# Decay attention and two gated layers: the attention's result in 32-column parts of the array, scores and state update in one burst, and a re-ordered plan

## The chip, the cores and the metric

The kernel runs on one core of one Trainium2 chip. A core has a matmul engine (TensorE, in the profile PE, its weight loads PEld), VectorE (DVE), ScalarE (ACT), GpSimd (POOL) and SyncE (SP), which issues the DMA transfers. The metric is the device time of one execution in microseconds; lower is better. Before the change the median of three runs is 1067.16 us (1066.91 to 1067.5).

## What is computed

Three stages follow each other, all in float32. The attention keeps a 48x48 state for each of 4 batches and 8 heads over 768 time steps:

```python
for t in range(S):
    kt, vt, rt = (k[:, :, t], v[:, :, t], r[:, :, t])
    cur = np.einsum('bhd,bhe->bhde', u[None] * kt, vt)
    y[:, :, t] = np.einsum('bhd,bhde->bhe', rt, state + cur)
    state = w[None, :, :, None] * state + np.einsum('bhd,bhe->bhde', kt, vt)
```

Its output, 3072 tokens of 384 numbers, goes through two gated layers with 1536 hidden columns:

```python
xn = x / rms * rms_g
x = silu(xn @ w_gate) * (xn @ w_val) @ w_out           # first layer
x = sigmoid(x @ w_gate2) * (x @ w_val2) @ w_out2       # second layer
```

The weights arrive as float64; the kernel turns them into pairs of float32 numbers itself.

## The kernel before, in words

**Attention.** The 768 steps of each batch are cut into 6 chunks of 128; a chunk of one batch is a tile, 24 tiles in all, taken chunk by chunk over the batches (tiles 0 to 3 are the first chunks, 20 to 23 the last). In a tile, keys and queries are scaled by powers of the decay (`kq`, `rq`, with `wk` and `wr`) and turned (`kT`, `rT`: in tiles 1 to 7 by TensorE, from tile 8 on by VectorE transposes and DMA). TensorE then runs four bursts, each with its own place in the order:
- `scores` (L498): 8 matmuls, for 4 pairs of heads, the two heads of a pair in the upper and lower 64 rows of the array. VectorE masks the two banks into `aa` (L502).
- `from_state` (L511), not in the first chunk: 4 matmuls of a head pair's `rT` with `zb`, a copy of the state `z` in which the two heads of a pair stand on a block diagonal (zeros elsewhere). ScalarE makes this copy in two pieces per tile (L539).
- `from_tile` (L518): 8 matmuls of `aa` with `vn`, into the same bank; VectorE adds `vc` and writes `x` (L521).
- `update` (L528), not in the last chunk: 8 matmuls of `kq` with `vn`, 48 columns of the array each, even heads in the left and odd heads in the right half. VectorE adds the product to `z` (L535) and multiplies it by `wc`.

Every float32 matmul of these leaves two records in the trace. `x` is then normalised, turned and split into a high and a low part, `xh` and `xl`.

**Gated layers.** A block is 512 tokens, six blocks per layer; a step is one block with 128 of the 1536 hidden columns, so 12 steps to a block and 144 in all. A step of the first layer has 9 + 9 matmuls of 512 columns for gate and value (L668 to L670) and 9 for the output (L695), 27 in all. ScalarE makes the gate (L675), VectorE the product (L677), ScalarE and VectorE split it into `hh` and `hl` (L679, L680). Step 11 is the last of block 0. Block 0 needs attention tiles 0 to 3, block 1 tiles 4 to 7, and so on. During block 0 the weights of each step are converted too (ScalarE L63, L68, L630; VectorE L77, L78, L633; GpSimd L84).

**What sets the order.** Nothing is scheduled on the chip. Class `Plan` places every task with an estimated duration, a due time, the data it reads and writes, and its PSUM banks, and writes each engine's instructions in the order that this gives. `DUE` sets when a tile of block 0, 1 and later blocks falls due (offset before its block, distance between tiles; a step is 3 units), `LEAD` how early the parts of a weight conversion are due, `STEP` how early a step's vector work is due. Tokens such as `("v", n)` name what tasks wait for. A task's token `("v", n)` stands for step n's value bank, and attention also names its ring of three value tiles `("v", 0)` to `("v", 2)`.

Of the kernel before, what the change touches and what calls it, by code (L numbers as in the profile page):

```python
# [11 lines left out]
AF = mybir.ActivationFunctionType  # L12
ALU = mybir.AluOpType
AX = mybir.AxisListType

P = 128
HS = 112
NPAIR = 4
# [6 lines left out]
DUE = (-59, 4), (-47, 4), (-42, 8)  # L25


LEAD = 15, 10, 7, 7, 8, 9
STEP = 4
# [69 lines left out]
class Plan:  # L99
# [46 lines left out]
    def run(self, start, fly):  # L146
# [18 lines left out]
        for _ in self.tasks:  # L165
            best = None
            for e, waiting in engines.items():

                first, could = None, []
                for n in waiting:  # L170
                    us, _, _, _, psum, dma = self.tasks[n]
# [3 lines left out]
                    at = at[e]  # L175
# [17 lines left out]
            at, n, e = best  # L193
# [33 lines left out]
def blocked(  # L227
# [31 lines left out]
    def ring(name, n, shape, dtype=F32):  # L259
        return [work.tile(shape, dtype, name=f"{name}{i}") for i in range(n)]  # L260
# [25 lines left out]

    zb = ring("zb", B, [HS, NPAIR, 2 * D])
# [38 lines left out]
    def setup():  # L326


        for t in zb:
            nc.gpsimd.memset(t, 0.0)  # L330
# [126 lines left out]
    def attention(i):  # L457
# [37 lines left out]
        def scores(*sp):  # L495
# [3 lines left out]
        add("T", 1.1, d + 3, scores, [(t, i2, n) for t in ("kT", "rT") for n in range(2)],  # L499
            [name("sp")], psum=[name(("sp", n)) for n in range(2)], gate=[("aa", n) for n in range(2)])  # L500
# [11 lines left out]
        if not first:  # L512
            add("T", 0.7, d + 5, from_state, [("rT", i2, n) for n in range(2)] + [("zb", b, 0), ("zb", b, 1)], [name("yp")],
                psum=[name("yp")], gate=[("x", i2)])
# [5 lines left out]
        add("T", 0.9, d + 6, from_tile, [("aa", 0), ("aa", 1), ("v", i3)], [name("yp")], psum=[name("yp")], gate=[("x", i2)])  # L520
        add("V", 0.47, d + 7, lambda yp: nc.vector.tensor_tensor(  # L521
            out=x[i2], in0=yp[:, :DM], in1=flat(vc[i2]), op=ALU.add), [name("yp"), ("vc", i2)], [("x", i2)], psum=[name("yp")])


        if not last:
            def update(up):
                for h in range(H):
                    nc.tensor.matmul(up[rows(h % 2), h // 2 * D:(h // 2 + 1) * D], kq_[:, h, :], vn[i3][:, h, :], start=True, stop=True)  # L528
            u3 = lambda up: up[:HS, :NPAIR * D].rearrange("p (q e) -> p q e", q=NPAIR)
            add("T", 0.55, d + 8, update, [("kq", i2), ("v", i3)], [name("up")], psum=[name("up")], gate=[("z", b)])  # L530
# [3 lines left out]
            else:  # L534
                add("V", 0.27, d + 9, lambda up: nc.vector.tensor_tensor(out=z[b], in0=u3(up), in1=z[b], op=ALU.add),  # L535
                    [name("up")], [("z", b)], psum=[name("up")])
                add("VG", (0.27, 0.55), d + 9, either(z[b], z[b], wc, ALU.mult), ["wc"], [("z", b)])
# [121 lines left out]
    def step(n, bi, f):  # L659
# [4 lines left out]
        def hidden(kind):  # L664
# [11 lines left out]
        add("T", 2.1, d + 1, hidden(1), xs + [("w", f, 1), ("g", n)], [("v", n)], psum=[("v", n)])  # L676
        add("V", 0.69, d + 1 - STEP, lambda ps: nc.vector.tensor_tensor(out=sg[n2], in0=ps, in1=sg[n2], op=ALU.mult),  # L677
            [("v", n)], [("sg", n2)], psum=[("v", n)])
# [268 lines left out]
```

## Time and profile before

| what | value |
|---|---|
| median of three runs | 1067.16 us |
| the profiled execution's own time | 1057.77 us |
| its span | 1056.0 us |
| mean granted TensorE clock | 0.992 |
| VectorE busy | 497.1 us |
| ScalarE busy | 357.9 us |
| GpSimd busy | 130.4 us |

The span runs from the first to the last instruction in the trace; 1.8 us of the execution lie around it. The share of busy time is a mean over three stages with different limits: the start until block 0 is done, the rest of the first layer with the other attention tiles between its steps, and the second layer, in which there is no attention. So each stage is read by itself below.

### The profile page before, as it was taken

The numbers are of one execution on the slowest core, as the hardware profiler recorded it, in microseconds if no ns is written. First come the engines' busy times: TensorE is split into PE (matmuls) and PEld (weight loads), VectorE is DVE, ScalarE is ACT, GpSimd is POOL, SyncE is SP. The second block draws the span as 40 slices with busy tenths as digits, with TensorE's granted clock in tenths as the row PEclk, the third lists the DMA queues.
The fourth block names the chain that finished last, engine by engine and source line by source line (L and its number), as shares of the span: only waits on it lengthen the run. The fifth ranks groups of instructions, "written<-read, shape, count | busy, mean of one in ns | idle before, by whom it ended". The sixth has DMA issues, their size and how long they took to land.

```text
span 1056.0 us, 14430 instructions
## 1 busy us (share of the span) xinstructions
PE 1034.9 (98%) x5474; PEld 870.4 (82%) x5474; DVE 497.1 (47%) x957; ACT 357.9 (34%) x750; POOL 130.4 (12%) x157
## 2 busy tenths in 40 slices
PE   7989999999999999999999999999999999999997
PEld 6867787888888888888888888888888888888886
DVE  8999984445664665554456422322322322222221
ACT  5566652223333333333455412221212212212121
POOL 4534430000121221011001000000000000000000
PEclk9989999999999999999999999999999999999998
DMA  9944755345565777543465300100100100000000
GB/s 199 254 95 131 135 121 108 60 77 136 123 153 124 158 156 163 133 126 96 145 192 165 120 1 1 60 1 1 61 1 1 60 1 1 30 1 5 27 1 34
DMA packets 213743, 91.10 MB, mean 86 GB/s; under 512 B 156576, under 2 KB 205984, under 8 KB 213664
## 3 DMA queue, kind: packets, MB, share of 16 engines
q1 hardware_dynamic: 213664, 90.08, 35.2%
q8 instruction: 45, 0.74, 0.3%
q14 instruction: 34, 0.28, 0.1%
HBM read 64.10 MB, written 25.95 MB: 85 GB/s over the span
## 4 chain that ended last, share of the span: by engine, by line
PE 89%; DVE 8%; issue 1%; ACT 1%; DMA 1%; SPq 0%; DVEq 0%; ACTq 0%
PE bank L695 27%; PE bank L668 19%; PE bank L669 18%; PE bank L670 18%; PE bank L518 3%; PE bank L498 2%; PE bank L511 1%; DVE wraw L78 1%; DVE w L633 1%; DVE wt L77 1%; DVE vc L466 1%; DVE aa L502 1%; DVE sg L314 1%; PE bank L528 1%; DVE hl L680 0%
## 5 line engine op out<-in xcount | busy, mean ns | idle before, releaser
L668 PE MATMUL bank<-xh,w 128*128 128x512 f32 x864 | 345.7, 400 | 0.6 <-ACT w L630 0.6
L669 PE MATMUL bank<-xl,w 128*128 128x512 f32 x864 | 342.1, 396 | 0.0
L670 PE MATMUL bank<-xh,w 128*128 128x512 f32 x864 | 341.9, 396 | 0.0
L677 DVE TENSOR_TENSOR sg<-bank,sg 128x512 f32<-128x512 f32 x144 | 99.4, 691 | 386.4 <-PE bank L670 386.1
L670 PEld LDWEIGHTS bank<-xh,w 128*128 128x128 f32 x864 | 162.5, 188 | 39.0 <-DVE w L633 0.5
L668 PEld LDWEIGHTS bank<-xh,w 128*128 128x128 f32 x864 | 162.7, 188 | 37.2 <-ACT w L630 1.0
L669 PEld LDWEIGHTS bank<-xl,w 128*128 128x128 f32 x864 | 162.7, 188 | 34.2
L675 ACT ACTIVATE sg<-bank 128x512 f32<-128x512 f32 x144 | 86.0, 598 | 303.5 <-PE bank L670 303.0
L679 ACT ACTIVATE hh<-sg 128x512 fp32r<-128x512 f32 x144 | 90.8, 631 | 228.8 <-DVE sg L677 228.7
L695 PE MATMUL bank<-w,hh 128*128 128x384 f32 x576 | 158.7, 337 | 0.0
L695 PE MATMUL bank<-hh,w 128*128 128x512 f32 x432 | 149.4, 399 | 0.8 <-ACT hh L679 0.8
L680 DVE TENSOR_TENSOR hl<-sg,hh 128x512 fp32r<-128x512 f32 x144 | 100.8, 700 | 62.6 <-ACT hh L679 62.5
L695 PEld LDWEIGHTS bank<-w,hh 128*128 128x128 f32 x576 | 105.1, 188 | 3.4
L695 PEld LDWEIGHTS bank<-hh,w 128*128 128x128 f32 x432 | 81.1, 188 | 20.5 <-ACT hh L679 1.2
L695 PE MATMUL bank<-w,hl 128*128 128x384 f32 x288 | 96.7, 336 | 0.0
L695 PE MATMUL bank<-hl,w 128*128 128x512 f32 x216 | 85.6, 396 | 1.9 <-DVE hl L680 1.9
L695 PEld LDWEIGHTS bank<-w,hl 128*128 128x128 f32 x288 | 54.1, 188 | 3.3 <-DVE hl L680 0.3
L84 POOL TENSOR_TENSOR wt<-wraw 128x384 int32<-128x384 int32 x36 | 32.5, 903 | 187.0 <-DVE wraw L78 110.2
L518 PEld LDWEIGHTS bank<-vn,aa 128*128 128x128 f32 x384 | 47.9, 198 | 5.9 <-DVE aa L502 3.9
L518 PE MATMUL bank<-vn,aa 128*128 128x48 f32 x384 | 48.3, 279 | 3.7 <-DVE aa L502 3.4
L63 ACT ACTIVATE wt<-wraw 128x384 f32<-128x384 f32 x72 | 39.7, 552 | 35.4 <-DMA wraw<-in_moe_w_gate_dram 11.3
L695 PEld LDWEIGHTS bank<-hl,w 128*128 128x128 f32 x216 | 40.6, 188 | 11.6 <-DVE hl L680 2.5
(121 smaller groups left out, 761.3 us busy)
## 6 DMA issues: line engine op xcount, KB each, us to landing
wraw<-in_moe_w_gate_dram SPq DMA_DIRECT2D x24, 384.0 KB, 4.0
wraw<-in_moe_w_val_dram SPq DMA_DIRECT2D x24, 384.0 KB, 4.3
wraw<-in_moe_w_out_dram SPq DMA_DIRECT2D x24, 384.0 KB, 4.5
parked<-wt SPq DMA_DIRECT2D x36, 192.0 KB, 2.7
wt<-parked SPq DMA_DIRECT2D x36, 192.0 KB, 2.4
kn<-in_k_dram SPq DMA_DIRECT2D x24, 192.0 KB, 4.4
rn<-in_r_dram SPq DMA_DIRECT2D x24, 192.0 KB, 4.5
vn<-in_v_dram SPq DMA_DIRECT2D x24, 192.0 KB, 3.4
```

Source lines behind the costliest of these rows:

```text
L63: nc.scalar.activation(t.bitcast(F32), raw[:, :, 1].bitcast(F32), AF.Abs, scale=2.0 ** -112, accum_out=total)
L84: nc.gpsimd.tensor_tensor(out=out, in0=raw[:, :, 1], in1=raw[:, :, 0], op=ALU.add)
L498: nc.tensor.matmul(sp[n][:, p * P:(p + 1) * P], kT[i2][rows(n), p, :], rT[i2][rows(n), p, :], start=True, stop=True)
L518: nc.tensor.matmul(yp[:, h * D:(h + 1) * D], aa[0][:, h % 2, h // 2, :], vn[i3][:, h, :], start=(first and h == 0), stop=True, skip_group_ ...
L668: nc.tensor.matmul(ps, whi[f][:, kind, ws], xh[b2][:, c, :], start=(c == 0), stop=False)
L669: nc.tensor.matmul(ps, whi[f][:, kind, ws], xl[b2][:, c, :], start=False, stop=False)
L670: nc.tensor.matmul(ps, wlo[f][:, kind, ws], xh[b2][:, c, :], start=False, stop=(c == KC - 1))
L675: add("A", 0.6, d - STEP, lambda g: nc.scalar.activation(sg[n2], g, gate), [("g", n)], [("sg", n2)], psum=[("g", n)])
L677: add("V", 0.69, d + 1 - STEP, lambda ps: nc.vector.tensor_tensor(out=sg[n2], in0=ps, in1=sg[n2], op=ALU.mult), [("v", n)], [("sg", n2)], ...
L679: add("A", 0.63, d + 1 - STEP, lambda: nc.scalar.activation(hh[n2], sg[n2], AF.Copy), [("sg", n2)], [("hh", n2)])
L680: add("VG", (0.69, 1.5), d + 1 - STEP, lambda e: by[e].tensor_tensor(out=hl[n2], in0=sg[n2], in1=hh[n2].bitcast(F32), op=ALU.subtract), [( ...
L695: nc.tensor.matmul(a[:, :rhs.shape[-1]], lhsT, rhs, start=(f == 0 and i == 0), stop=(f == NF - 1 and i == 2))
```

## The change

`from_state` and `from_tile` become one task, `result` (L525 and L530). Each of their matmuls is cut into four, one for each quarter of the tile's 128 steps, so that each takes 32 columns of the array. The state's share no longer uses a block diagonal: each head is a matmul with 48 rows from `z` itself, even heads in the upper and odd heads in the lower 64 rows. That makes 32 + 32 matmuls in place of 4 + 8, into two banks in place of one (even heads, odd heads); VectorE adds `vc` in two halves (L536). The copy `zb`, its zeroing on GpSimd and its ScalarE copies go. `scores` and `update` become one task, which takes three banks at once. The step's value token is renamed `("value", n)`, so it is no longer the same name as attention's value tiles. When two engines could start a task at the same moment, the plan now takes the one with the earlier due time first. `DUE`, `LEAD` and `STEP` have other numbers, and the plan's estimates for the new bursts are 1.4, 0.95, 1.6 and 1.1 us.

```diff
-DUE = (-59, 4), (-47, 4), (-42, 8)
-LEAD = 15, 10, 7, 7, 8, 9
-STEP = 4
+DUE = (-75, 4), (-36, 5), (-41, 6)
+LEAD = 17, 20, 18, 15, 14, 18
+STEP = 12
+Y_US, S_US = (1.4, 0.95), (1.6, 1.1)
...
-                _, n = min((self.tasks[n][1], n) for at, n in could if at <= first + 1e-9)
-                if best is None or first < best[0]:
-                    best = (first, n, e)
+                due, n = min((self.tasks[n][1], n) for at, n in could if at <= first + 1e-9)
+                if best is None or (first, due) < best[:2]:
+                    best = (first, due, n, e)
...
+        def both(*ps):
+            scores(*ps[:2])
+            if not last:
+                update(ps[2])
...
-        def from_state(yp):
-            y3 = yp[:, :DM].rearrange("p (q e) -> p q e", q=NPAIR)
-            for p in range(NPAIR):
-                nc.tensor.matmul(y3[:, p, :], rT[i2][:HS, p, :], zb[b][:, p, :], start=(p == 0), stop=False, skip_group_check=True)
-        def from_tile(yp):
-            for h in range(H):
-                nc.tensor.matmul(yp[:, h * D:(h + 1) * D], aa[0][:, h % 2, h // 2, :], vn[i3][:, h, :],
-                                 start=(first and h == 0), stop=True, skip_group_check=True)
+        quarters = [slice(t, t + P // 4) for t in range(0, P, P // 4)]
+        def result(*yp):
+            for p in range(NPAIR if not first else 0):
+                for ts in quarters:
+                    for n in range(2):
+                        nc.tensor.matmul(yp[n][ts, p * D:(p + 1) * D], rT[i2][rows(n), p, ts], z[b][rows(n), p, :],
+                                         start=(p == 0), stop=False, skip_group_check=True)
+            for n in range(2):
+                for p in range(NPAIR):
+                    for ts in quarters:
+                        nc.tensor.matmul(yp[n][ts, p * D:(p + 1) * D], aa[0][:, n, p, ts], vn[i3][:, 2 * p + n, :],
+                                         start=(first and p == 0), stop=True, skip_group_check=True)
...
-            for n in range(2):
-                add("A", 0.25, d + 10, lambda n=n: nc.scalar.activation(
-                    zb[b][rows(n), :, n * D:(n + 1) * D], z[b][rows(n)], AF.Copy), [("z", b)], [("zb", b, n)])
...
-        add("T", 2.1, d + 1, hidden(1), xs + [("w", f, 1), ("g", n)], [("v", n)], psum=[("v", n)])
+        add("T", 2.1, d + 1, hidden(1), xs + [("w", f, 1), ("g", n)], [("value", n)], psum=[("v", n)])
```

How the order moves is shown at three places. The first is TensorE ahead of the first gated step. Before, tile 4's result (L511, L518) is followed by tile 5's scores (L498), and the first step (L668) starts behind them; its two halves then have tile 5's and 6's attention between them:

```order
L511 MATMUL bank_77<-zb_125,rT_116 128x96 x4
L518 MATMUL bank_78<-vn_100,aa_117 128x48 x8
L498 MATMUL bank_80<-rT_116,kT_114 128x128
...
L668 MATMUL bank_79<-xh_128,w_446 128x512
...
L324 MATMUL bank_74<-ident,kq_102 112x128 x4
L324 MATMUL bank_75<-ident,rq_104 112x128 x4
L528 MATMUL bank_76<-vn_99,kq_102 48x48 x8
L518 MATMUL bank_77<-vn_101,aa_117 128x48 x8
L498 MATMUL bank_78<-rT_115,kT_113 128x128
```

After the change, tile 4's scores, update (L502) and result (L525, L530) are the last attention ahead of the first step (L678), and five more steps follow it with no attention between them:

```order
L502 MATMUL bank_73<-vn_100,kq_102 48x48 x8
L525 MATMUL bank_77<-z_120,rT_115 32x48
...
L530 MATMUL bank_77<-vn_100,aa_117 32x48 x16
L530 MATMUL bank_74<-vn_100,aa_117 32x48 x16
L574 MATMUL bank_75<-ident,x_119 128x128 x3
L678 MATMUL bank_79<-xh_124,w_435 128x512
```

Tiles 5, 6 and 7 moved from the start of block 0 into its steps 6 to 11, and tiles 8 and 9, which stood in steps 6 to 10, moved behind step 11's output.

The second place is TensorE around tile 14, deep in the first layer. Before, its scores, its two result bursts (both into bank_80) and its update stand apart, with matmuls of the gated layers (left out) between them:

```order
L498 MATMUL bank_79<-rT_115,kT_113 128x128
L498 MATMUL bank_78<-rT_115,kT_113 128x128
...
L511 MATMUL bank_80<-zb_126,rT_115 128x96 x4
...
L518 MATMUL bank_80<-vn_101,aa_117 128x48 x8
...
L528 MATMUL bank_78<-vn_101,kq_102 48x48 x8
```

After, such a tile has two places, one with scores and update, one with the result in two banks (tile 12's, then tile 13's):

```order
L525 MATMUL bank_79<-z_120,rT_115 32x48
L525 MATMUL bank_78<-z_120,rT_115 32x48
...
L530 MATMUL bank_79<-vn_99,aa_117 32x48 x16
L530 MATMUL bank_78<-vn_99,aa_117 32x48 x16
...
L498 MATMUL bank_79<-rT_116,kT_114 128x128
L498 MATMUL bank_80<-rT_116,kT_114 128x128
...
L502 MATMUL bank_78<-vn_100,kq_103 48x48 x8
```

Four entries into the row of gated matmuls became two for each tile.

The third place is VectorE up to the product of step 11 (L677, after L687). Before, 316 rows stand ahead of it, and just ahead are a state update, a conversion and a transpose for tile 9:

```order
L475 TENSOR_REDUCE cf_107<-vc_105 128x8
L466 TENSOR_TENSOR z_122<-z_122,wc 112x192
L553 SCALAR_TENSOR_TENSOR x_119<-x_119,rms_112,g_bc 128x384
L77 TENSOR_SCALAR wt_147<-wt_147 128x384
L446 STREAM_TRANSPOSE vc_106<-x_119 128x384
L78 SCALAR_TENSOR_TENSOR wraw_143<-wraw_143,wt_147 128x384
L677 TENSOR_TENSOR sg_133<-bank_76,sg_133 128x512
```

After, 284 rows stand ahead of the same product, and what is just ahead belongs to tile 7's split and tile 8's first transposes:

```order
L580 TENSOR_TENSOR xl_127<-bank_80,xh_125 128x3x128
L446 STREAM_TRANSPOSE kn_97<-kq_102 128x384
L446 STREAM_TRANSPOSE rn_95<-rq_104 128x384
L80 TENSOR_SCALAR wt_143<-wt_143 128x384
L475 TENSOR_REDUCE cf_107<-vc_105 128x8
L81 SCALAR_TENSOR_TENSOR wraw_139<-wraw_139,wt_143 128x384
L687 TENSOR_TENSOR sg_129<-bank_76,sg_129 128x512
```

Most of tiles 8 and 9 moved behind the product, and some multiplications moved to GpSimd.

## Rows read from the trace of the kernel before

**Rows 1.** The page: busy time of each engine, share of the span, instructions.

```profile
PE 1034.9 (98%) x5474; PEld 870.4 (82%) x5474; DVE 497.1 (47%) x957; ACT 357.9 (34%) x750; POOL 130.4 (12%) x157
```

**Rows 2.** By stretch: length, busy PE, PEld, DVE, ACT, POOL; clock, DMA share, GB/s.

```profile
25.00:50.00 25.00, 24.08 (x261) 20.95 (x260) 24.69 (x58) 15.01 (x40) 12.99 (x15) 1.00 1.15 248
50.00:75.00 25.00, 20.11 (x135) 17.09 (x134) 22.14 (x46) 14.85 (x39) 7.20 (x8) 0.86 0.56 140
...
11.00:163.00 152.00, 141.66 (x995) 117.34 (x995) 142.52 (x297) 94.90 (x238) 65.38 (x62) 0.97 0.71 158
163.00:599.00 436.00, 436.00 (x2297) 354.88 (x2296) 235.12 (x449) 159.41 (x340) 59.28 (x69) 1.00 0.54 132
```

**Rows 3.** TensorE's waits: who waited for whom, us in total, times, longest.

```profile
PE bank L518 <- DVE aa L502: 3.4, 4, 2.2
```

**Rows 4.** TensorE's timeline at the start: start, us, engine, line, operation, count [idle before].

```profile
29.57 1.76 PE L518 MATMUL bank<-vn,aa 128*128 128x48 f32 x14 [0.24 <-DVE aa L502]
...
60.33 3.13 PE L518 MATMUL bank<-vn,aa 128*128 128x48 f32 x14 [2.18 <-DVE aa L502]
```

**Rows 5.** Timeline of VectorE and TensorE at the end of step 11.

```profile
155.68 0.69 DVE L677 TENSOR_TENSOR sg<-bank,sg 128x512 f32<-128x512 f32 x1 [0.84 <-PE bank L670]
...
162.24 0.39 PE L695 MATMUL bank<-hh,w 128*128 128x512 f32 x1
```

**Rows 6.** TensorE's timeline: each burst with a gated matmul ahead and the second behind.

```profile
279.46 0.39 PE L695 MATMUL bank<-hh,w 128*128 128x512 f32 x1
279.69 1.03 PE L511 MATMUL bank<-zb,rT 112*128 112x96 f32 x8
...
280.81 0.39 PE L669 MATMUL bank<-xl,w 128*128 128x512 f32 x1
...
282.44 0.40 PE L670 MATMUL bank<-xh,w 128*128 128x512 f32 x1
282.68 1.88 PE L518 MATMUL bank<-vn,aa 128*128 128x48 f32 x16
...
284.69 0.39 PE L669 MATMUL bank<-xl,w 128*128 128x512 f32 x1
...
288.42 0.40 PE L695 MATMUL bank<-hh,w 128*128 128x512 f32 x1
288.75 0.56 PE L528 MATMUL bank<-vn,kq 128*48 128x48 f32 x16
...
289.58 0.39 PE L669 MATMUL bank<-xl,w 128*128 128x512 f32 x1
...
295.41 0.40 PE L695 MATMUL bank<-hh,w 128*128 128x512 f32 x1
295.74 1.16 PE L498 MATMUL bank<-rT,kT 48*128 48x128 f32 x16
...
297.17 0.40 PE L669 MATMUL bank<-xl,w 128*128 128x512 f32 x1
```

**Rows 7.** By line and shape: busy us, mean ns of one, idle before.

```profile
L518 PE MATMUL bank<-vn,aa 128*128 128x48 f32 x384 | 48.3, 279 | 3.7 <-DVE aa L502 3.4 <-DVE rms L549 0.2
...
L528 PE MATMUL bank<-vn,kq 128*48 128x48 f32 x320 | 11.4, 216 | 0.0
...
L502 DVE TENSOR_TENSOR aa<-bank,mask 128x512 f32<-128x512 f32 x48 | 31.5, 682 | 12.6 <-PE bank L498 12.6
...
L553 DVE SCALAR_TENSOR_TENSOR x<-x,rms,g_bc 128x384 f32<-128x384 f32 x24 | 16.7, 695 | 5.6 <-POOL rms L465 5.6
...
L521 DVE TENSOR_TENSOR x<-bank,vc 128x384 f32<-128x384 f32 x24 | 13.3, 553 | 37.3 <-PE bank L518 37.3
...
L475 DVE TENSOR_REDUCE cf<-vc 128x8 f32<-128x384 f32 x24 | 12.9, 538 | 0.0
...
L535 DVE TENSOR_TENSOR z<-bank,z 112x192 f32<-112x192 f32 x16 | 5.5, 350 | 1.9 <-PE bank L528 1.9
...
L549 DVE TENSOR_SCALAR rms<-ss 128x1 f32<-128x1 f32 x24 | 3.6, 148 | 7.6 <-ACT vc L544 7.3
...
L539 ACT ACTIVATE zb<-z 48x192 f32<-48x192 f32 x40 | 14.4, 360 | 14.8 <-DVE z L466 8.9 <-PE bank L511 5.6
```

More of the change, by code (lines that the diff above doesn't have):

```diff
@@ L285, in blocked @@
     x, z = ring("x", 2, [P, DM]), ring("z", B, [HS, NPAIR, D])
-    zb = ring("zb", B, [HS, NPAIR, 2 * D])
     xh, xl = ring("xh", 2, [P, KC, N], F32R), ring("xl", 2, [P, KC, N], F32R)
@@ L326, in setup @@
     def setup():
-        for t in zb:
-            nc.gpsimd.memset(t, 0.0)
         nc.vector.memset(o[0], 0.0)
@@ L498, in scores, with update @@
                     nc.tensor.matmul(sp[n][:, p * P:(p + 1) * P], kT[i2][rows(n), p, :], rT[i2][rows(n), p, :], start=True, stop=True)
-        add("T", 1.1, d + 3, scores, [(t, i2, n) for t in ("kT", "rT") for n in range(2)],
-            [name("sp")], psum=[name(("sp", n)) for n in range(2)], gate=[("aa", n) for n in range(2)])
+        def update(up):
+            for h in range(H):
+                nc.tensor.matmul(up[rows(h % 2), h // 2 * D:(h // 2 + 1) * D], kq_[:, h, :], vn[i3][:, h, :], start=True, stop=True)
+        def both(*ps):
+            scores(*ps[:2])
+            if not last:
+                update(ps[2])
+        more = [] if last else [name("up")]
+        add("T", S_US[last], d + 3, both, [(t, i2, n) for t in ("kT", "rT") for n in range(2)] + ([] if last else [("kq", i2), ("v", i3)]),
+            [name("sp")] + more, psum=[name(("sp", n)) for n in range(2)] + more, gate=[("aa", n) for n in range(2)])
         for n in range(2):
@@ L505, in attention @@
                 [name("sp")], [("aa", n)], psum=[name(("sp", n))])
-        def from_state(yp):
-            y3 = yp[:, :DM].rearrange("p (q e) -> p q e", q=NPAIR)
-            for p in range(NPAIR):
-                nc.tensor.matmul(y3[:, p, :], rT[i2][:HS, p, :], zb[b][:, p, :], start=(p == 0), stop=False, skip_group_check=True)
-        if not first:
-            add("T", 0.7, d + 5, from_state, [("rT", i2, n) for n in range(2)] + [("zb", b, 0), ("zb", b, 1)], [name("yp")],
-                psum=[name("yp")], gate=[("x", i2)])
@@ new lines, in attention @@
+        banks = [name(("yp", n)) for n in range(2)]
+        add("T", Y_US[first], d + 6, result, [("aa", 0), ("aa", 1), ("v", i3)] + ([] if first else [("rT", i2, 0), ("rT", i2, 1), ("z", b)]),
+            [name("yp")], psum=banks, gate=[("x", i2)])
+        for n in range(2):
+            add("V", 0.27, d + 7, lambda yp, n=n: nc.vector.tensor_tensor(
+                out=half_of(x[i2].rearrange("p (h d) -> p h d", h=H), n), in0=yp[:, :NPAIR * D].rearrange("p (q d) -> p q d", q=NPAIR),
+                in1=half_of(vc[i2], n), op=ALU.add),
+                [name("yp"), ("vc", i2)], [("x", i2)], psum=[banks[n]])
@@ L525, in attention @@
         if not last:
-            def update(up):
-                for h in range(H):
-                    nc.tensor.matmul(up[rows(h % 2), h // 2 * D:(h // 2 + 1) * D], kq_[:, h, :], vn[i3][:, h, :], start=True, stop=True)
             u3 = lambda up: up[:HS, :NPAIR * D].rearrange("p (q e) -> p q e", q=NPAIR)
-            add("T", 0.55, d + 8, update, [("kq", i2), ("v", i3)], [name("up")], psum=[name("up")], gate=[("z", b)])
             if first:
@@ L536, in attention @@
                     [name("up")], [("z", b)], psum=[name("up")])
-                add("VG", (0.27, 0.55), d + 9, either(z[b], z[b], wc, ALU.mult), ["wc"], [("z", b)])
-            for n in range(2):
-                add("A", 0.25, d + 10, lambda n=n: nc.scalar.activation(
-                    zb[b][rows(n), :, n * D:(n + 1) * D], z[b][rows(n)], AF.Copy), [("z", b)], [("zb", b, n)])
+                add("VG", (0.27, 0.6), d + 9, either(z[b], z[b], wc, ALU.mult), ["wc"], [("z", b)])
         t = ss[i2]
```

7 lines of the change are left out of this document (2 added, 5 removed).

## The prediction, made before the changed kernel ran

> **What bounds the kernel now.** I read the busy table first: TensorE is busy 98% of the span, every other engine under half [rows 1]. That alone only says that TensorE's stream matters, so I read it by stretch. From 163 to 599 us TensorE is busy 436.00 of 436 us at full granted clock, with VectorE at 54% [rows 2]: every microsecond taken out of TensorE's work there comes off the end. The second layer, from 599 us on, has no attention, and the change doesn't touch it. The start is different: from 11 to 163 us, where block 0's weights are converted and tiles 0 to 9 are worked, TensorE is idle 10.3 of 152 us while VectorE is busy 142.5, 94% [rows 2]. TensorE's waits name VectorE's `aa` first [rows 3], and after such a wait of 2.18 us fourteen records took 3.13 us where they took 1.76 before; the stretch shows a granted clock of 0.86, so part of it lay at the 1.2 GHz level [rows 2, 4]. So there are two bounds: VectorE's work until step 11, TensorE's afterwards. The sum is made for each.
>
> **TensorE's bursts, before.** In a dense row the gated matmuls start 0.233 us apart: 289.58 to 295.41 us holds 25 such intervals [rows 6]. A burst costs the time from the gated matmul ahead of it to the second one behind, less two intervals (0.47). That gives 0.88 for `from_state`, 1.78 for `from_tile`, 0.69 for `update` and 1.29 for `scores` [rows 6], 4.64 us a tile. The window from 163 to 599 holds 14 scores, 14 results and 8 updates: 14 x 3.95 + 8 x 0.69 = 60.8 us.
>
> **The result burst, after.** No row shows a matmul of 32 columns, so I bound it. `update` is the nearest: 16 records on two column halves in 0.56 us, the last 0.216 long, so starts are (0.56 - 0.216) / 15 = 0.023 us apart, and each half takes 0.046 for a record [rows 6, 7]. `from_tile`, which fills the array, needs (1.88 - 0.279) / 15 = 0.107 a record. So parts of the array do work side by side. With 0.046 a record in every part, `from_tile`'s 64 records on four parts take 16 rounds, 0.74 us, and `from_state`'s 64 on eight parts (four of columns, two of rows) 8 rounds, 0.37 us. Around its records `update` pays 0.69 - 16 x 0.023 = 0.32; I add the same: 1.45 us, against 2.66 now, and 1.06 against 1.78 in the first chunk. The low end scales the round with the columns, 32 for 48: 0.74 + 0.32 = 1.06 us. The high end holds the pace of starts at 0.023, the fastest in the trace, whatever the number of parts: 128 x 0.023 + 0.32 = 3.27 us. I take 1.45, since the two-part row shows a pace set by the part and not by the stream; both ends stay for the range.
>
> The Trainium skill has a rule against this change: "TensorE: Matmul & The Clock Gate", section "Wait — 56ns, not 53.3ns?", says that matmul starts never come closer than about 25 ns, however small the matmul. The row above, 0.023, lies just below it and was measured with two parts only, so it doesn't decide. By the rule the burst would be an estimated 128 x 0.025 + 0.32 = 3.5 us. The same page's section "Measured speedup vs the span model" has matmuls on different tiles start about 4 ns apart, which no row here shows for more than two parts.
>
> **Scores with update.** One entry and one exit go; inside, I charge the update's records (0.36) and one change of shape, 0.1, an estimate from its 0.32 around: 0.46 instead of 0.69, a gain of 0.23 where a tile has an update. If the change of shape costs as much as leaving and entering, the gain is 0.
>
> **Sum after step 11.** Behind step 11's output there stand now 16 tiles, not 14 (tiles 8 and 9 were moved there), with 12 updates: 16 x 1.29 + 12 x 0.46 + 16 x 1.45 = 49.3 us. Against 60.8 that is -11.5 us. The gated matmuls in this part are the same ones.
>
> **Sum to step 11.** VectorE's product of step 11 starts at 155.68, and the step's last output matmul at 162.24 [rows 5]. Ahead of that product VectorE's order has 29 instructions fewer: 4 masks of 0.682; 22 of 384 elements, between 0.538 and 0.695, say 0.59; 5 of 192 elements at 0.36, as `z` in the row; 4 tiny ones of 0.148; while `x` is 16 halves of 0.35 in place of 10 of 0.553, which is even [rows 7]. Together 2.7 + 13.0 + 1.8 + 0.6 = 18 us. Most is tiles 8 and 9, put off to where VectorE has slack; some went to GpSimd, busy 65 of 152 us there [rows 2]. VectorE wasn't fed all the time, so I don't take all 18: 13 us, with step 11's output ending near 149. TensorE can keep that: without the two tiles (2 x 3.95 + 4 updates x 0.69 = 10.7) and with the savings of eight tiles (4 x 1.21 + 4 x 0.72 + 8 x 0.23 = 9.6) its own work would allow some 20 us. What is late next is again VectorE.
>
> **Edits I cost at nothing.** ScalarE's `zb` copies, 40 of 0.36 us, lie on an engine busy a third of the span [rows 1, 7]; uncovered they would cost 0.72 us a tile. The zeroing on GpSimd comes before its first work. The state's addition must now wait for the result burst that reads `z`; behind it on VectorE wait products and splits of the gated steps, and TensorE for those. The plan places it behind the burst, and `z` is next needed four tiles later, so nothing is charged; each time it were late it would cost up to the 0.35 of its own length. The combined burst needs three banks at once and waits for `kq` and the values too; both are ready before the turned keys are. The renamed token, the tie rule and the due times act through the order alone and are in the two sums. Weight loads are issued earlier, through queues that are already full at 25 to 50 us (248 GB/s, DMA share above 1 [rows 2]); that is one reason not to take all 18 us.
>
> **Forecast.** -11.5 - 13 = -24.5 us, so the profiled execution would go from 1057.77 to 1033. The runs lie 9.4 us above the profiled one; I keep that distance: 1067.16 - 24.5 = 1043 us.
>
> **Rivals.**
> - *The start gives nothing.* VectorE, the loads or a wait for `hl` hold step 11 at 162 us; for: VectorE is 94% busy there and the new order packs six steps with no attention to fill gaps. Then only -11.5 stays: 1056 us.
> - *The start becomes TensorE's.* GpSimd takes enough off VectorE; TensorE's 20.3 us and some 6 of its 10.3 idle come out: -26 - 11.5, 1030 us. Against: the VectorE sum.
> - *Slower: the stream of matmuls is the bound.* Starts stay 0.023 us apart; the burst costs 3.27, the part after step 11 16 x (1.29 + 3.27) + 12 x 0.46 = 78.5, +17.7, while the start keeps -10 of its gain: 1075 us. It decides from a burst of about 2.8 us upwards. For: no row shows more than two parts at once. By the 25 ns of the Trainium skill ("TensorE: Matmul & The Clock Gate", section "Wait — 56ns, not 53.3ns?") an estimated 4 us would come on top.
> - *The parts do not overlap beyond what was.* A burst near 2.66 us as now: 16 x 3.95 + 5.5 - 60.8 = +7.9, with -10 at the start: 1065 us, no change that can be told.
>
> **Chances.** Forecast 0.57 (own range 1034 to 1051), start gives nothing 0.15, start becomes TensorE's 0.10, slower 0.13, no change 0.05. Under 0.2%, some 2.1 us, a measurement of this kernel can't tell a change. So faster 0.82, the same 0.05, slower 0.13. The range 1027 to 1058 holds the first three cases and leaves out the last two.
>
> **What would show it.** After the change TensorE's timeline should show, between gated matmuls, a result burst of 1.2 to 1.7 us from the gated matmul ahead to the second behind, less 0.47, with 128 records; 2.8 or more would make the forecast wrong, and so would `scores` with `update` above 1.98. Step 11's last output matmul should start near 149 us, with tiles 0 to 7 ahead of it; at 160 or later the start has failed. VectorE should be over 90% busy up to there, with TensorE's waits naming `hl`, `aa` or weights. From there to the end of the first layer TensorE should show no idle time; new waits of TensorE for `z`, `x` or a bank there would say that the two-burst tile has been placed too tightly. The second layer should take as long as before.

## The result, and the profile after

The changed kernel takes 1039.24 us (median of four runs, 1038.28 to 1040.48) against 1067.04 for the kernel before on the same chip (1060.29 to 1067.5): a ratio of 0.9755, 95% interval 0.9714 to 0.9795. The prediction was 1043 us, range 1027 to 1058. Faster, and in the range; the sections below ask which of its terms held.

The profiled execution took 1038.28 us, its span 1036.6. Its busy line, to be held against [rows 1]:

```profile
PE 1013.8 (98%) x7746; PEld 841.5 (81%) x7746; DVE 494.6 (48%) x967; ACT 342.0 (33%) x710; POOL 140.5 (14%) x167
```

TensorE has 2272 matmul records more and is busy 21 us less. By stretch (length, busy PE, PEld, DVE, ACT, POOL; clock, DMA share, GB/s), to be held against [rows 2]; the border is now at 150 us, where step 11 ends:

```profile
20.00:30.00 10.00, 9.48 (x191) 8.24 (x188) 9.88 (x23) 6.64 (x17) 5.91 (x6) 0.72 1.08 244
...
11.00:150.00 139.00, 127.16 (x1458) 100.10 (x1457) 128.22 (x266) 85.53 (x212) 60.70 (x59) 0.93 0.59 147
150.00:580.00 430.00, 430.00 (x4108) 343.74 (x4107) 247.24 (x490) 153.03 (x325) 75.51 (x85) 1.00 0.60 142
```

As before, TensorE has no idle time in the second part, and VectorE is 92% busy in the first. The end of step 11 on both engines [rows 5]:

```profile
146.55 0.68 DVE L687 TENSOR_TENSOR sg<-bank,sg 128x512 f32<-128x512 f32 x1
...
149.71 0.39 PE L705 MATMUL bank<-hh,w 128*128 128x512 f32 x1
```

The start gave 162.24 - 149.71 = 12.5 us. From there to the same matmul of step 71, the end of the first layer, it is 430.27 us against 436.88 before: 6.6 us. The second layer takes 448.6 us in both. Together 19.1 us, which is the difference of the spans, 19.4, but for a rest at the edges. The part at the start holds against this first profile of the kernel before; against its second one (`before_again`, below) it is 170.37 - 149.71 = 20.7 us.

TensorE's bursts deep in the first layer, with a gated matmul ahead and the second behind, as in [rows 6]:

```profile
278.65 0.40 PE L705 MATMUL bank<-hh,w 128*128 128x512 f32 x1
278.98 1.16 PE L498 MATMUL bank<-rT,kT 48*128 48x128 f32 x16
280.07 0.56 PE L502 MATMUL bank<-vn,kq 128*48 128x48 f32 x16
280.56 0.50 PE L705 MATMUL bank<-hh,w 128*128 128x512 f32 x1
280.90 0.40 PE L705 MATMUL bank<-hl,w 128*128 128x512 f32 x1
...
283.23 0.40 PE L680 MATMUL bank<-xh,w 128*128 128x512 f32 x1
283.56 0.80 PE L525 MATMUL bank<-z,rT 48*32 48x48 f32 x64
284.29 0.89 PE L530 MATMUL bank<-vn,aa 128*32 128x48 f32 x64
285.11 0.50 PE L678 MATMUL bank<-xh,w 128*128 128x512 f32 x1
285.45 0.39 PE L679 MATMUL bank<-xl,w 128*128 128x512 f32 x1
```

By the rule of the prediction, scores with update cost 280.90 - 278.65 - 0.467 = 1.78 us (1.75 was predicted), and the result costs 285.45 - 283.23 - 0.467 = 1.75 us (1.45 was predicted). TensorE's waits (who for whom, us in total, times, longest), to be held against [rows 3]; all lie before step 11:

```profile
PE bank L530 <- issue: 2.7, 2, 2.1
PE bank L326 <- DVE kq L466: 2.5, 2, 1.8
PE bank L412 <- DVE o L316: 1.7, 1, 1.7
PE bank L678 <- ACT w L640: 1.6, 1, 1.6
...
PE bank L530 <- DVE aa L512: 0.7, 2, 0.5
```

### The profile page after: what moved, and what is told of

It is laid out like the page before. It is cut to its first block, busy times and chain, and to the rows that moved or that the text cites. A ratio compares the mean times of both kernels' runs of the same rounds, so it can differ in the third digit from the quotient of the medians.

```text
span 1036.6 us, 18973 instructions
## 1 busy us (share of the span) xinstructions
PE 1013.8 (98%) x7746; PEld 841.5 (81%) x7746; DVE 494.6 (48%) x967; ACT 342.0 (33%) x710; POOL 140.5 (14%) x167
## 3 DMA queue, kind: packets, MB, share of 16 engines
q8 instruction: 62, 1.02, 0.4%
## 4 chain that ended last, share of the span: by engine, by line
PE 90%; DVE 5%; DMA 2%; ACT 1%; SPq 1%; issue 1%; DVEq 0%; ACTq 0%
PE bank L705 28%; PE bank L678 19%; PE bank L679 19%; PE bank L680 19%; PE bank L498 2%; PE bank L530 2%; DMA wraw<-in_moe_w_val_dram 1%; PE bank L525 1%; DVE w L643 1%; DMA wraw<-in_moe_w_gate_dram 1%; PE bank L502 1%; DVE aa L512 1%; SPq L307 1%; DVE vc L466 1%; DVE wraw L81 1%
## 5 line engine op out<-in xcount | busy, mean ns | idle before, releaser
L678 PE MATMUL bank<-xh,w 128*128 128x512 f32 x864 | 344.8, 399 | 2.2 <-ACT w L640 1.6
L687 DVE TENSOR_TENSOR sg<-bank,sg 128x512 f32<-128x512 f32 x144 | 99.4, 690 | 393.5 <-PE bank L680 391.5
L678 PEld LDWEIGHTS bank<-xh,w 128*128 128x128 f32 x864 | 162.8, 188 | 39.3 <-ACT w L640 2.1
L705 PE MATMUL bank<-hh,w 128*128 128x512 f32 x432 | 151.6, 402 | 0.1
L87 POOL TENSOR_TENSOR wraw<-wraw 128x384 int32<-128x384 int32 x36 | 38.6, 1080 | 62.7 <-DVE wraw L81 42.7
L81 DVE SCALAR_TENSOR_TENSOR wraw<-wraw,wt 128x384 int32<-128x384 int32 x72 | 41.7, 587 | 1.4
```

Of the source, the lines that this page charges most:

```text
L81: yield nc.vector.scalar_tensor_tensor(out=high, in0=high, scalar=-(1 << 31), in1=t, op0=ALU.bitwise_and, op1=ALU.bitwise_or)
L87: nc.gpsimd.tensor_tensor(out=out, in0=raw[:, :, 1], in1=raw[:, :, 0], op=ALU.add)
L678: nc.tensor.matmul(ps, whi[f][:, kind, ws], xh[b2][:, c, :], start=(c == 0), stop=False)
L705: nc.tensor.matmul(a[:, :rhs.shape[-1]], lhsT, rhs, start=(f == 0 and i == 0), stop=(f == NF - 1 and i == 2))
```

## The experiments

Three things were open: whether the parts of the array or the order brought the gain; what holds the start; and why the medians lie 27.8 us apart where the profiles show 19.4. The table has all runs; each ratio is to the kernel before as timed beside that kernel. "Step 11" is the start of its last output matmul in the timeline, "to 71" the time from there to that of step 71. What each kernel is stands in its section.

| kernel | median us | ratio, 95% interval | step 11 | to 71 |
|---|---|---|---|---|
| before, beside the changed kernel; places from its first profile, a run of 1057.77 | 1067.04 | | 162.24 | 436.88 |
| before_again | 1066.19, one run | | 170.37 | 436.88 |
| changed | 1039.24 | 0.9755 (0.9714 to 0.9795) | 149.71 | 430.27 |
| e_whole | 1067.36 | 1.0008 (0.9984 to 1.0032) | 153.95 | 455.17 |
| e_halves | 1039.99 | 0.9765 (0.9743 to 0.9786) | 147.11 | 432.29 |
| e_mixed | 1037.32 | 0.9733 (0.9713 to 0.9754) | 150.02 | 428.81 |
| e_order | 1064.96 | 0.9995 (0.9973 to 1.0017) | 163.40 | 444.97 |
| e_bursts | 1049.82 | 0.9859 (0.9828 to 0.9890) | 167.00 | 423.57 |
| e_token | 1049.95 | 0.9853 (0.9824 to 0.9881) | 167.66 | 423.57 |
| e_wait | 1080.67 | 1.0146 (1.0120 to 1.0172) | 192.38 | 428.93 |
| e_split | 1041.63 | 0.9780 (0.9749 to 0.9811) | 149.84 | 433.19 |
| e_noshift | 1035.72 | 0.9712 (0.9673 to 0.9751) | 146.68 | 430.73 |
| e_before_warm | 1061.63 | 0.9963 (0.9938 to 0.9988) | 164.29 | 436.89 |
| e_mixed_warm | 1038.15 | 0.9734 (0.9709 to 0.9759) | 151.63 | 429.05 |

"To 71" depends on how many tiles an order leaves behind step 11 (16 in the changed kernel, 14 in the kernel before, 15 in e_order and e_wait), so it is compared only between kernels with the same number, or with the tile counted. "Step 11" depends on TensorE's clock in the start too, which differs from profile to profile, so small differences in it say little.

### The width of the parts: e_whole, e_halves, e_mixed

```diff
e_whole:   -quarters = [slice(t, t + P // 4) for t in range(0, P, P // 4)]
           +quarters = [slice(0, P)]
e_halves:  +quarters = [slice(t, t + P // 2) for t in range(0, P, P // 2)]
e_mixed:   +halves = [slice(t, t + P // 2) for t in range(0, P, P // 2)]
           -                for ts in quarters:
           +                for ts in halves:
```

In e_mixed only the state's share (L525) goes in halves. The order of the tasks is the changed kernel's in all three. Expected of e_whole:

> The result in whole matmuls of 128 columns, as before the change, but in the changed order and with the bursts in their new places: the column split alone is undone. Theory 'the gain behind step 11 is the parts': tile part 16 starts of 0.107 = 1.71 us, state part 8 rounds of 0.112 = 0.90, burst 2.6 to 2.9 against 1.75 us; 16 tiles behind step 11 and some of the first 4 give 14 to 20 us: 1053 to 1060, and the first GLU step's output stands near 150 us as in the changed kernel. Rival 'it is the order and the token': 1039 to 1042, bursts hidden or as short as with the parts.

Measured: 1067.36 us, as before the change. Its result burst (columns as above) takes 282.44 - 278.96 - 0.467 = 3.01 us:

```profile
278.96 0.40 PE L680 MATMUL bank<-xh,w 128*128 128x512 f32 x1
279.29 1.10 PE L525 MATMUL bank<-z,rT 48*128 48x48 f32 x16
280.31 1.99 PE L530 MATMUL bank<-vn,aa 128*128 128x48 f32 x16
282.12 0.48 PE L678 MATMUL bank<-xh,w 128*128 128x512 f32 x1
282.44 0.40 PE L679 MATMUL bank<-xl,w 128*128 128x512 f32 x1
```

"To 71" is 24.9 us longer than in the changed kernel; 16 bursts of 3.02 instead of 1.75 are 20.3 of it. The rest is at three of these bursts, after which TensorE ran at half clock for about 3.5 us (granted clock 0.83 in the stretches 340 to 350, 450 to 460 and 490 to 500 us), as here:

```profile
339.26 1.09 PE L525 MATMUL bank<-z,rT 48*128 48x48 f32 x16
340.29 1.99 PE L530 MATMUL bank<-vn,aa 128*128 128x48 f32 x16
342.10 0.58 PE L678 MATMUL bank<-xh,w 128*128 128x512 f32 x1
342.47 0.63 PE L679 MATMUL bank<-xl,w 128*128 128x512 f32 x1
342.90 0.63 PE L680 MATMUL bank<-xh,w 128*128 128x512 f32 x1
```

Gated matmuls are 0.43 us apart there and not 0.233. No stretch behind step 11 shows this in the changed kernel. So the order without the parts brings nothing, and the parts are the gain's condition. This burst is longer than the two of the kernel before together (2.66 us by the prediction), since the block diagonal is gone as well, which is 16 x 0.36 = 5.8 us; e_order, below, has the old bursts and brings nothing either. The miss is the time, which came out above the 1053 to 1060: the burst was 3.02, not 2.6 to 2.9, step 11 came 4.2 us later, and the clock's falls were not foreseen.

Expected of the other two, first e_mixed, then e_halves:

> The state's share of a result goes in halves of the array (2 row groups of 48 x 2 column halves, 32 starts of 64 columns), the tile's own share stays in quarters (64 starts of 32 columns); plan and order of tiles are unchanged. Theory 'stream': the state part's 0.73 us in the changed kernel is set by the number of its 64 starts, some 8 to 11 ns each, not by its parts; with 32 starts on four parts it takes 0.37 to 0.50, the burst 1.40 to 1.55 us, and 20 bursts give about 5 us: 1034 (1032 to 1037). Theory 'parts': a part of 48 rows x 32 columns is worth as much as its share of the array, halves are half as many parts as quarters and the state part goes to about 0.9 us: 1043. If the stalls of TensorE inside bursts near the start (2.13 us, no semaphore named) come from fetching its instructions, they get shorter, as a tile has 64 instructions fewer (32 matmuls and their 32 weight loads).

> Both shares of the result in halves of the array (64 columns): 32 starts on 2 parts for the tile's own share, 32 on 4 parts for the state's. Theory 'stream': tile part 0.85 to 0.95 us by its two parts (0.82 now), state part 0.37 to 0.50 (0.73 now): the burst is 1.50 to 1.65 us against 1.75, and time about 1036 (1034 to 1039). Theory 'parts': two columns instead of four cost the tile part 1.7 us and the state part 0.9: burst 2.9, 1058. Theory 'fetch': half the result's instructions, so that TensorE's unexplained stalls in the bursts near 31 and 39 us (0.55 and 2.13 us) go, 1 to 3 us before step 11, with the clock's fall behind them.

```profile
283.53 0.68 PE L526 MATMUL bank<-z,rT 48*64 48x48 f32 x32
284.14 0.89 PE L531 MATMUL bank<-vn,aa 128*32 128x48 f32 x64
284.96 0.50 PE L679 MATMUL bank<-xh,w 128*128 128x512 f32 x1
```

```profile
281.84 0.68 PE L525 MATMUL bank<-z,rT 48*64 48x48 f32 x32
282.45 1.14 PE L530 MATMUL bank<-vn,aa 128*64 128x48 f32 x32
283.52 0.50 PE L678 MATMUL bank<-xh,w 128*128 128x512 f32 x1
```

The first fence is e_mixed (burst 1.62 us in the mean), the second e_halves (1.87). Neither theory has the numbers. From one share's start to the next start, divided by the records on one part:

| share | whole | halves | quarters |
|---|---|---|---|
| tile's, 128 rows | 1.81 / 16 = 0.113, 1 part | 1.07 / 16 = 0.067, 2 parts | 0.82 / 16 = 0.051, 4 parts |
| state's, 48 rows | 1.02 / 8 = 0.128, 2 parts | 0.61 / 8 = 0.076, 4 parts | 0.73 / 8 = 0.091, 8 parts |

These are means over a whole share, the change to the next share included. Narrower parts take less each, and up to four work side by side; on eight each record takes longer than on four. Eight parts and 64 starts come together in the state's share, so which of the two makes it slow is not shown. e_halves loses 16 x 0.124 = 2.0 us behind step 11 and gets 2.6 at the start of its profile, the same time in all. So "stream" is right that the state's share is faster with 32 starts than with 64 (0.61 against 0.73 us), and wrong that 32 starts would keep the pace of the 64 (0.011 us a start). For the tile's share quarters are best, for the state's halves: e_mixed saves 0.126 us a burst, 20 bursts 2.5 us, and measures 1.9 us under the changed kernel, 1036.57 to 1037.73 against 1038.28 to 1040.48; the two were not timed side by side. It is the fastest of the full kernels here.

### Order, token and bursts apart: e_bursts, e_order, e_token, e_wait, e_split

```diff
e_bursts:  the changed kernel with the old order and token
           -DUE = (-75, 4), (-36, 5), (-41, 6)        +DUE = (-59, 4), (-47, 4), (-42, 8)
           -LEAD = 17, 20, 18, 15, 14, 18             +LEAD = 15, 10, 7, 7, 8, 9
           -STEP = 12                                 +STEP = 4
           -if best is None or (first, due) < best[:2]:   +if best is None or first < best[0]:
           -hidden(1), ..., [("value", n)], ...       +hidden(1), ..., [("v", n)], ...
e_token:   as e_bursts, but with ("value", n)
e_wait:    the changed kernel, with ("v", n)
e_order:   the kernel before, with the new DUE, LEAD, STEP, tie rule and ("value", n)
```

> The bursts alone: parts of 32 columns and merged bursts as in the changed kernel, but the old order of tasks (old due times, leads, step, tie rule) and the old token. Theory 'parts': with whole matmuls the new order brought nothing (1067 against 1066), so the gain is the parts; each result burst behind step 11 is 1.75 us against 2.68 before, 14 of them, scores and update 1.78 against 1.98, 11 of them: 15 us, and 3 to 6 at the start, with the clock's falls behind result bursts gone (up to 8 us): 1038 to 1046. Theory 'the start belongs to the order': the first GLU step's last output stays near 158 to 162 us as in the kernel before, and time is 1046 to 1052.

> The order alone: the kernel before with the new due times, leads, step, tie rule and the new token; bursts separate and whole as before. Theory 'parts': the first GLU step's output comes some 8 us earlier, as in the kernel with whole matmuls (153.95 against 162.24), but two more tiles of 4.6 us lie behind it, and nothing is gained: 1062 to 1068. Theory 'order': 1050 to 1058. Theory 'clock': between step 12 and step 71 any stretch at half clock begins right behind a result burst of whole matmuls.

> Parts, merged bursts and the new token, with the old due times, leads, step and tie rule: between the kernel with the bursts alone (1049.8) and the changed one (1039). With the old token and the new due times TensorE stood 29 us for kq and time was 1081, so token and due times don't add up. Theory 'token': it frees the order by itself, 1038 to 1044, the first GLU step's output before 158 us. Theory 'only both': 1046 to 1053, as the bursts alone.

> The changed kernel with the old token between the second hidden burst and VectorE's product (the false wait kept), all else as changed. Theory 'nothing': the wait ended under TensorE's own work, 1038 to 1040. Rival 'the wait held the start': VectorE stands until the bank's second writer is through, 12 steps before step 11 of up to 0.7 us each lose some of it: 1041 to 1046.

The bursts alone bring 16 us (1049.8). Behind step 11, where 14 tiles stand as before, it is 436.88 - 423.57 = 13.3 us, near the 15 expected; the start brings nothing to speak of, 167.00 lying between the two profiles of before. The order alone brings nothing, e_order and e_whole agree on that. In e_order step 11 comes 7.0 us earlier than in the second profile of the kernel before, whose clock also fell to half in the start (below), but the part behind step 11, with one tile more, takes 8.1 us longer. No half clock came behind step 11 in e_order, so its third theory had no case; in the start the granted clock was 0.50 from 20 to 30 us. The token alone brings nothing either, e_token equals e_bursts. But in the changed kernel, going back to the old token costs 41 us: a prediction of "nothing" to +7 that failed by far. The trace of e_wait shows it at TensorE:

```profile
74.16 1.10 PE L326 MATMUL bank<-ident,kq 128*112 128x128 f32 x4 [23.30 <-DVE kq L466]
```

and over the stretch around it TensorE is busy less than half the time (columns as in the first stretches above):

```profile
41.00:117.00 76.00, 36.48 (x569) 28.74 (x570) 65.79 (x137) 46.18 (x122) 31.11 (x33) 0.57 0.51 131
```

Gate bursts start at 43.49 us, but the first step's value burst stands behind tile 7's update, at 108.95: with one name for two things the plan takes it for a writer of attention's values and puts it after their readers. With the old due times these readers come early enough, with the new ones they come late. So the false wait is one of the plan, not of the chip, and it is worth nothing or 41 us, by the due times.

The merged burst, undone (e_split):

```diff
-        def both(*ps):
-            scores(*ps[:2])
-            if not last:
-                update(ps[2])
...
+        add("T", 1.1, d + 3, scores, [(t, i2, n) for t in ("kT", "rT") for n in range(2)],
+            [name("sp")], psum=[name(("sp", n)) for n in range(2)], gate=[("aa", n) for n in range(2)])
...
+            add("T", 0.55, d + 8, update, [("kq", i2), ("v", i3)], [name("up")], psum=[name("up")], gate=[("z", b)])
```

> Scores and update as two tasks again, the update due five later, the result in parts, the rest as changed. By the bursts: 1.28 and 0.69 us apart against 1.78 together, 11 tiles behind step 11 and some 8 ahead of it: +2 to +4 us, 1041 to 1043. Rival 'the order around it matters more': the first GLU step's output moves by more than 3 us to either side, and time with it.

1041.63, 2.4 us more, though the two were not timed side by side and their runs overlap (1039.28 to 1044.29). Step 11 stands where it stood (149.84), and "to 71" is 2.9 longer: the price of the bursts, as expected.

### What holds the start: e_noshift

```diff
 def float_bits(nc, raw, t, clamp=True):
-    yield nc.vector.tensor_scalar(out=t, in0=t, scalar1=3, scalar2=None, op0=ALU.logical_shift_left)
+    if not clamp:
+        yield None
+    else:
+        yield nc.vector.tensor_scalar(out=t, in0=t, scalar1=3, scalar2=None, op0=ALU.logical_shift_left)
```

It leaves out the shift of the weights' bits, 36 instructions of VectorE from 11 to 150 us.

> The shift of the weights' bits on VectorE is left out, so the weights are not the reference's; the planned order is the changed kernel's. In its trace these are 36 instructions of 0.469 us from 11 to 150 us, 16.3 us. Theory 'VectorE bounds the start': the first GLU step's output comes 8 to 14 us before 149.7, time 1025 to 1032. Rival 'TensorE bounds it': it is busy some 127 of those 139 us, so at most 3 us come out, 1036 to 1039. Rival 'loads': the transfers fill the queues up to 50 us and nothing moves there.

```profile
11.00:150.00 139.00, 127.20 (x1469) 100.20 (x1471) 118.14 (x232) 85.00 (x213) 57.24 (x60) 0.95 0.59 149
```

VectorE went from 128.22 to 118.14 us, and step 11 came 3.0 us earlier, not 8 to 14. TensorE is busy 127 us as before. From 50 us to step 11, first in the changed kernel, then in e_noshift:

```profile
50.00:149.70 99.70, 94.43 (x844) 73.48 (x843) 91.47 (x183) 61.71 (x151) 39.81 (x37) 0.98 0.40 105
50.00:146.60 96.60, 95.42 (x855) 74.79 (x855) 83.93 (x156) 62.83 (x156) 37.02 (x38) 0.99 0.44 112
```

TensorE's idle time went from 5.3 to 1.2 us there. So in the changed kernel's order VectorE does not bound the start by itself; behind 50 us TensorE's own time is next at once. The rival had it: at most 3 us. The clock was a little higher too (0.95 against 0.93 from 11 to 150 us), so not all of the 3.0 need be VectorE's.

The stall that the page calls "issue" shows in this kernel too. Two lines of the changed kernel, then two of e_noshift, in which both stand in tile 4's result:

```profile
38.39 0.96 PE L530 MATMUL bank<-vn,aa 128*32 128x48 f32 x45
41.48 0.45 PE L530 MATMUL bank<-vn,aa 128*32 128x48 f32 x19 [2.13 <-issue]
```

```profile
39.30 0.74 PE L533 MATMUL bank<-vn,aa 128*32 128x48 f32 x45
43.24 0.45 PE L533 MATMUL bank<-vn,aa 128*32 128x48 f32 x19 [3.20 <-issue]
```

Both stop behind the 45th of the same 64 records, though a microsecond apart in time; so a place in the program seems to decide, and not an event on another engine. In e_mixed TensorE is not stopped within that burst, but behind it:

```profile
39.41 1.15 PE L531 MATMUL bank<-vn,aa 128*32 128x48 f32 x64
42.68 0.55 PE L575 MATMUL bank<-ident,x 128*128 128x128 f32 x3 [2.13 <-DVE x L564]
```

`x` is late there anyway, so the stall costs little where it stands. That is what theory "fetch" missed: "issue" is gone from TensorE's waits in e_halves, e_mixed and e_whole, as it said, but in e_mixed step 11 comes no earlier (150.02). Nor do fewer records keep the stall away: e_mixed with ten more matmuls near the start (e_mixed_warm, below) has it again in tile 4's result:

```profile
43.60 0.38 PE L533 MATMUL bank<-vn,aa 128*32 128x48 f32 x7 [2.74 <-issue]
```

### Why before's runs lie above its profile: before_again, e_before_warm, e_mixed_warm

> The kernel before, once more with a profile: its timed spans run from 1060 to 1067 us at a mean granted clock of 0.978 to 0.989, its profiled one was 1056.0 at 0.992. Theory 'clock behind bursts': at a clock below 0.99 this trace shows stretches of 3 to 4 us at half clock behind step 11 that the first trace doesn't have, each beginning behind a result burst, about 1.7 us lost in each, and their sum is the time above 1056. Rival: the time is lost before step 11, in the loads and VectorE's work, and the clock is low there because TensorE waits.

The second profile of the kernel before, 1066.19 us, shows the same 436.88 us behind step 11, without any half clock there: the theory fell. The time is lost before step 11, whose output comes at 170.37, 8.1 us later; the rival had the place, though not the loads and VectorE as what takes the time. Two stretches of the first profile, then of the second:

```profile
20.00:30.00 10.00, 9.52 (x115) 8.33 (x114) 9.45 (x22) 9.18 (x26) 4.94 (x6) 1.00 1.23 232
30.00:40.00 10.00, 9.76 (x118) 8.72 (x117) 9.87 (x24) 4.40 (x12) 4.69 (x6) 1.00 1.19 232
```

```profile
20.00:30.00 10.00, 10.00 (x66) 9.25 (x66) 5.42 (x12) 5.08 (x14) 4.06 (x3) 0.50 0.91 199
30.00:40.00 10.00, 10.00 (x69) 9.25 (x69) 6.51 (x13) 3.86 (x9) 3.52 (x4) 0.50 0.56 117
```

The same program is bound by VectorE in the one and by TensorE at the 1.2 GHz level in the other, where it has no idle time and gets through 66 records in 10 us instead of 115. The first profile was a rare one: the 17 runs beside e_whole have spans of 1059.8 to 1067.2 us at a mean clock of 0.989 to 0.978, none as short as 1056.0 at 0.992. In the changed kernel the clock is 0.72 from 20 to 30 us and 1.00 from 30 to 40.

To see whether TensorE's idle time ahead makes the clock fall, it was filled:

```diff
         def update(up):
             for h in range(H):
                 nc.tensor.matmul(up[rows(h % 2), ...], kq_[:, h, :], vn[i3][:, h, :], start=True, stop=True)
+            for _ in range(10 if i == 0 else 0):
+                nc.tensor.matmul(up[:, 384:], ident, ident, start=True, stop=True)
```

> The kernel before with ten matmuls of the identity with itself behind tile 0's update, into columns nobody reads: they fill TensorE's wait of 2.84 us for kq (13.2 to 16.1 us). The planned order is the same. In two profiles of the kernel before, one went through 20 to 47 us at full clock (step 11's output at 162.2, span 1056.0), one at half clock from 17 to 46 us (170.4, 1064.4). Theory 'the wait makes the clock fall': with the wait filled the clock stays up in most runs, 1057 to 1061. Rival 'the long bursts of whole matmuls keep it down': 1063 to 1068, as the kernel before.

> The kernel with the state's share in halves (1037.3), with the same ten matmuls behind tile 0's update. Its granted clock was 0.67 from 11 to 20 us and 0.95 from 20 to 30 us. Theory 'the wait makes the clock fall': 1 to 3 us off, 1034 to 1036. Rival 'VectorE's and TensorE's waits hold the start anyway': 1037 to 1038.

The kernel before gains 6.1 us against its runs on the same chip (1067.76), with work added, just less than the theory wanted. In its profile the clock stays up from 20 us on:

```profile
20.00:30.00 10.00, 9.36 (x113) 8.07 (x112) 9.58 (x22) 8.89 (x25) 5.57 (x6) 1.00 1.18 232
30.00:40.00 10.00, 9.70 (x115) 8.58 (x116) 9.86 (x24) 4.22 (x12) 4.89 (x6) 1.00 1.01 217
```

The granted clock of its 12 runs is 0.99 in the median, against 0.982 without the ten matmuls, but the runs go from 1057.21 to 1068.63, so the clock still falls in some of them. With the wait filled it falls less often; whether the idle time did it, or the ten matmuls by moving all that follows, these runs don't separate. e_mixed gains nothing by it (1038.15 against 1037.32): with the ten matmuls TensorE goes on at 17.0 us, a microsecond after the wait that they fill, and its clock from 20 to 30 us was 0.95 without them.

## Why the prediction was right, and where it was not

- **Faster, by parts that work side by side: held.** e_whole takes the parts away, and the whole gain with them, 5.8 us of it by a burst longer than that of before; e_order, with the old bursts, gains nothing either. The slower rival, starts never closer than 0.023 us, is out: the state's 64 records start in 0.73 us, 0.011 apart, and neighbours in the tile's share 0.007. By that the rule of about 25 ns of the Trainium skill ("TensorE: Matmul & The Clock Gate", section "Wait — 56ns, not 53.3ns?") doesn't hold for records that start on different parts of the array. That each record is an instruction of its own fits the instruction queue, which moved 17 packets of 16 KB more for 4543 records more (matmuls and loads), 61 bytes a record against 51 in the kernel before. The trace of the kernel before had spoken against this rival already: within `update`'s burst the records start in pairs, 0.007 us apart, which fits one for each half of the array, and mostly 0.045 from pair to pair. So the 0.023 that the prediction calls the fastest pace in the trace is a mean of closer and wider starts, and single starts were closer before the change. The first pair of `update` at 288.75 us, two records in 0.25 us:

```profile
288.75 0.25 PE L528 MATMUL bank<-vn,kq 128*48 128x48 f32 x2
```

- **-11.5 us behind step 11: -6.6.** The term that was mis-sized is the result burst, 1.45 predicted, 1.75 measured; 16 x 0.30 = 4.8 us of the 4.9 missing. Within it the tile's share came near (0.74, measured 0.82), the state's did not: 0.37 for 8 rounds of 0.046, measured 0.73; around them it pays 0.20 (1.75 - 0.82 - 0.73), not 0.32. The step "each part at update's pace, however many parts" failed between four parts and eight. Scores with update came as said, 1.75 against 1.78.
- **-13 us at the start: -12.5, in part by luck, and for a reason that is half of it.** The -12.5 is against the rare first profile; against the second it is -20.7, while the changed kernel's own profile was at half clock for part of its start (0.72 from 20 to 30 us). The rows behind the 13 were VectorE's, and TensorE was given room by the parts in the same sum. VectorE's busy time ahead of the product of step 11 fell from 142.83 to 128.50 us, 14.3 where the sum had 18. The runs say that the parts alone don't move the start (e_bursts 167.00). The order does so even with whole matmuls (e_whole 153.95), but only with the parts is that not lost again behind step 11. "What is late next is again VectorE" failed: without the shifts, some 16 us of VectorE's work, 3 us came (e_noshift).
- **"The runs lie 9.4 us above the profiled one; I keep that distance": failed.** In the second profile it was 8.1 us lost at half clock in the start of the kernel before, which the first profile happened not to show, and the changed kernel's four runs lie within 2.2 us of its profile. That gave 8 us more than the forecast, and the part behind step 11, above all the state's share, took 5 back: 1039 instead of 1043. That the forecast lies within 4 us of the result is luck to that extent, as two misses of opposite sign stand in it.
- **Edits at nothing: held.** TensorE has no idle time behind step 11 and waits for no `z`, `x` or bank there. The token was rightly put down to the order, though what it is worth in this order, 41 us, was not seen.
- **The signs named ahead.** VectorE over 90% busy (92%), tiles 0 to 7 ahead of step 11, second layer unchanged: all there. The result burst lay just outside 1.2 to 1.7. Of TensorE's waits `aa` and weights were named; "issue" and `kq`, the two longest, were not, and `hl`, which was named, doesn't occur.

What stays open: what stops TensorE within tile 4's result, since no row names a releaser; whether the state's share is slow by its eight parts or its 64 starts; and why the clock falls in some runs and not in others after the same work.

## What to carry to other kernels

Small float32 matmuls whose weights change each time gained here from being cut into column parts of the array, up to four parts at a time: 1.81 us became 0.82, while 64 records on eight parts took longer than 32 on four. An order and a burst's length have to be tried together, as each alone gave 0 or 16 of 28 us, and a shared token gave 0 or 41. Before adding a run's distance from its profile to a forecast, see which stage of a second profile it is in.

## What the runs showed of the hardware

- A record of 128 rows takes 0.113 us alone on the array, 0.067 on each of two parts, 0.051 on each of four; with 48 rows 0.128, 0.076 and 0.091 on two, four and eight. These are means over a share, the change to the next share included.
- TensorE stops without a semaphore in tile 4's result: for 2.1 to 3.2 us behind 1213 matmul and load records of the trace in the changed kernel, e_wait, e_noshift and e_mixed_warm, for 0.6 us behind as many in e_token, and for 2.0 us behind 1211 in e_split, whose order differs. In e_bursts it stops for 2.9 us behind 1979, among gated matmuls. All six kernels with 128 records to a result have such stalls; of those with 96 to a result e_mixed_warm has one and e_mixed none, and those with fewer have none. In this stretch the transfers fill the DMA engines, and over the whole execution the instruction queue moves 62 packets of 16 KB in place of 45:

```profile
q1 hardware_dynamic: 7191, 3.93, 100.5%
q8 instruction: 3, 0.05, 1.4%
```

  These are the queues from 30 to 45 us of the changed kernel (packets, MB, share of 16 engines). A count that decides, and full queues, fit a late fetch of instructions; that was argued, not shown, and in the kernel before the queues are as full from 30 to 45 us (113.8%) with no such stop. The Trainium skill ("Runtime: NRT & Kernel Launch", section "Instruction fetch mechanics") has the next page fetched while the current one runs and its cost mostly hidden; no run here takes the transfers away to tell.
- After 3.0 us of whole 48-column matmuls TensorE's clock fell to its half level in three of 16 cases, after 1.75 us of the same work in parts in none.
